# Fourier layer: the feature transform folded a second time, its tables unpacked on ScalarE, and a finer split of the weights

## The chip, the cores and the metric

The kernel runs on one core of a Trainium2 chip. The metric is device time in microseconds (us) of one launch, the median of several runs. Engines are named as in the profile: PE is TensorE (PEld its weight loads), DVE is VectorE, ACT is ScalarE, POOL is GpSimd, SP issues most of the transfers.

## What is computed

Local-global attention on 2 x 8 heads of 768 tokens, then two feed-forward layers. The second one has a two-dimensional Fourier transform ahead of it, of which only the real part is kept; that part is what the change touches.

```python
def _moe2_ref(x, w_ch1, w_ch2):
    X = np.fft.fft(x, axis=1)          # over 768 tokens
    X = np.fft.fft(X, axis=2)          # over 512 features
    u = x + np.real(X).astype(np.float32)
    mu = np.mean(u, axis=-1, keepdims=True)
    var = np.mean((u - mu) ** 2, axis=-1, keepdims=True)
    un = (u - mu) / np.sqrt(var + 1e-06)
    ch = np.maximum(un @ w_ch1, 0.0) @ w_ch2
    return u + ch
```

## The kernel before

**Number format.** Most products run on pairs of fp32r tiles: an operand is split into a rounded part (`h`, `hi`) and a rest (`l`, `lo`), and a product of two operands takes three matmuls: high x high, high x low, low x high. Weights are split in `w_split`: ACT casts 128x1024 values to `wh` (L196), POOL subtracts to get `wo` (L200). For the first 16 chunks POOL does it in four pieces of 256 columns, later in two of 512.

**The main stream.** `ffn` runs over chunks c of 128 hidden units; a block of tokens takes 16 chunks. Chunk c needs 12 products of 512 columns into `ps_h` (L225, "the h pass of c"), then ACT makes `gh` (L232) and DVE makes `gl` (L233), and one chunk later 12 products into four `ps_acc` (L248, "the acc pass of c", which takes `gh`, `gl`, `wh`, `wo` of c). The h pass of c+1 stands ahead of the acc pass of c. At the end of a block DVE adds the accumulators to x (L268).

**Side work.** `drive` advances the main stream step by step (four steps a chunk) and, at a rate given as a number, a chain of side generators; a `yield` is one piece of it. Chunks 16 to 31 carry four transposes and `fft_tables`, chunks 32 to 47 `fft(0)` and the norms, chunks 48 to 63 `fft(1)` and `unit_tokens`. The code's order is not the engines' order: a scheduler places each instruction on its engine, and an instruction that it believes ready may stand ahead of others that were written earlier. On an engine the order is then fixed: an instruction that waits holds all behind it.

**The Fourier part.** `fft(b)` folds the token axis (sums and differences of tokens j and 768-j), and `fold` folds the feature axis once (m and 512-m): 257 cosine terms into `ee`, 256 sine terms into `oo`, split into high and low by ACT (L779) and DVE (L784). Then come products with the token tables `c1` and `s1` (L825 to L849, 386 or 384 columns), split again into `pt` (`fpt`) and `qt` (`fqt`), and products with the feature tables `c2` (258 columns, L862, with one of the sign row `sgn`, L864) and `s2` (256 columns, L875), which sum over two halves `dd` of the features. `pcos` runs four times in an `fft`, the sine products three times. ACT copies the sine result (`qc`, L878); DVE forms `dm` and `sm` (L881, L882) and adds them to x. `c1`, `s1`, `c2`, `s2`, `alt` and `sgn` are loaded by transfers that POOL issues (L739, L742, L751).

Of the kernel before, what the change touches and what calls it, by code (L numbers as in the profile page):

```python
# [39 lines left out]
class Prog:  # L40
# [147 lines left out]
    def w_split(self, c):  # L188
        if c >= PLAIN:
            return  # L190
        nc = self.nc
# [4 lines left out]
        keep(nc.scalar.copy(hi, raw))  # L196

        n = 2 * D // (4 if c < NF else 2)
        for z in range(0, 2 * D, n):
# [553 lines left out]
    def fft(self, b):  # L753
# [11 lines left out]
        oo = fp.tile([P, 2, 3, 256], FR, tag="oo", bufs=1, name=f"oo{b}")  # L765
        ee, oo = [ee[:, z] for z in range(2)], [oo[:, z] for z in range(2)]

        def fold(rows, E, O, h, l, i):
            if O is False:
                f = self.qkb[i % 2][:, 1024:1024 + K1]  # L770
                nc.vector.tensor_tensor(f[0:rows, 1:256], E[:, 1:256], E[:, 511:256:-1], ALU.add)
                nc.vector.tensor_copy(f[0:rows, 0:257:256], E[:, 0:257:256])
                nc.vector.memset(f[0:rows, 257:258], 0.0)
            else:
                f = self.vb[i % 2][:, 1024:1024 + K1]
                nc.vector.tensor_tensor(f[0:rows, 1:256], E[:, 1:256], E[:, 511:256:-1], ALU.subtract)
                nc.vector.memset(f[0:rows, 0:1], 0.0)
            n = K1 if O is False else 256
            nc.scalar.copy(h, f[0:rows, 0:n])  # L779
            if l is None:  # L780
                f, l = f[32:33], h[32:33]
                nc.vector.tensor_tensor(l, f[:, 0:n], l.bitcast(F32), ALU.subtract)
            else:
                nc.vector.tensor_tensor(l, f[0:rows, 0:n], h.bitcast(F32), ALU.subtract)  # L784

        em = fp.tile([P, KP], FR, tag="em", bufs=1, name=f"em{b}")[:, 0:K1]
        for i in range(3):
            E, O = (self.qkb[z][:, (i % 2) * D:(i % 2 + 1) * D] for z in range(2))
            nc.vector.tensor_tensor(E, A[i], Bp[i], ALU.add)
            fold(P, E, False, ee[0][:, i, :], ee[1][:, i, :], i)  # L790
            yield
            nc.vector.tensor_tensor(O, A[i], Bp[i], ALU.subtract)
            fold(P, O, True, oo[0][:, i, :], oo[1][:, i, :], i)
            if i == 1:
                fold(P, xm, False, em, None, 0)
            yield
        if b == 1:
            for _ in range(6):
                yield
        c1, s1, c2, s2 = ([ct[n + "0"], ct[n + "1"]] for n in ("c1", "s1", "c2", "s2"))  # L800
        pt = fp.tile([P, 2, 2, JP], FR, tag="fpt", bufs=1, name=f"fpt{b}")[:, :, :, 0:J1]
# [53 lines left out]
            nc.vector.tensor_tensor(l, pp[:, 0:384], h.bitcast(F32), ALU.subtract)  # L855
            yield

        def pcos(out, at):
            n = 0
            for dd in range(2):  # L860
                for x, y in PS:
                    nc.tensor.matmul(out, lhsT=at(pt[x][:, dd, :]), rhs=c2[y][:, dd, :], start=n == 0, stop=False)  # L862
                    n += 1
            nc.tensor.matmul(out, lhsT=at(pr), rhs=ct["sgn"], start=False, stop=True)  # L864

        for i in range(3):
# [5 lines left out]
            n = 0
            for dd in range(2):
                for x, y in PS:
                    nc.tensor.matmul(qs[:, 0:256], lhsT=qt[x][:, dd, js], rhs=s2[y][:, dd, :], start=n == 0, stop=n == 5)  # L875
                    n += 1
            qc = self.dist[i % 2][:, 2 * K1:3 * K1]
            nc.scalar.copy(qc[:, 0:256], qs[:, 0:256])  # L878
            sm = self.dist[0][:, 0:K1]
            dm = self.dist[0][:, K1:2 * K1]  # L880
            nc.vector.tensor_tensor(dm, pc[:, 0:K1], qc, ALU.subtract)  # L881
            nc.vector.tensor_tensor(sm, pc[:, 0:K1], qc, ALU.add)  # L882
# [417 lines left out]
```

## Time and profile before

| | us |
|---|---|
| median of 3 runs (lowest, highest) | 658.80 (657.76, 659.46) |
| the profiled execution | 660.58 |
| span of the profiled execution | 658.8 |
| PE busy in it | 644.6 |

The profile is of one execution. Its span is from the first to the last instruction; some 1.8 us of the execution lie outside. Busy times of an engine count overlapping instructions once. A matmul's record is longer than the distance to the next one, since matmuls are pipelined: distances between starts are the measure of what one costs.

### The profile page before, as it was taken

The page shows a single profiled execution, that of the slowest core. Times are in us where ns is not written, and L with a number is a line of the kernel's source. Part 1 is how long each engine was busy: PE and PEld are TensorE (multiplying, and loading weights), DVE is VectorE, ACT ScalarE, POOL GpSimd, SP SyncE. Part 2 cuts the span into 40 slices and gives each one's busy share as a digit, 9 for nine tenths or more (in the row PEclk, how much of TensorE's full clock was granted, in tenths as well). Part 3 has the DMA queues.
Part 4 walks back from the last instruction along what each step waited for, and adds up shares of the span by engine and source line. Part 5 has one row for each costly group of instructions (what it writes and reads, how often), then busy time and mean ns, then how long its engine had stood idle before and what let it go on. Part 6 is the DMA issues. An engine that isn't in the chain of part 4 may idle for free.

```text
span 658.8 us, 9571 instructions
## 1 busy us (share of the span) xinstructions
PE 644.6 (98%) x3442; PEld 535.3 (81%) x3442; DVE 425.0 (65%) x784; ACT 298.2 (45%) x584; POOL 345.6 (52%) x360
## 2 busy tenths in 40 slices
PE   6998999999999999999999999999999999999996
PEld 5887777888888888888888888888888888888885
DVE  5799778887839434387467766387556544464544
ACT  5787774554344434335334433235543443233420
POOL 4130235787986554566347665165484664446610
PEclk8999999999999999999999999999999999999999
DMA  7578816788995968666463961112111111011003
GB/s 255 195 302 290 283 44 196 231 262 246 319 352 182 303 221 269 218 198 232 157 202 119 316 223 68 63 65 96 33 64 65 65 64 65 7 58 64 2 2 132
DMA packets 33866, 107.51 MB, mean 163 GB/s; under 512 B 3920, under 2 KB 7952, under 8 KB 30736
## 3 DMA queue, kind: packets, MB, share of 16 engines
q1 hardware_dynamic: 31104, 102.23, 45.7%
q0 software_dynamic: 2416, 3.65, 2.1%
q10 hardware_dynamic: 288, 0.92, 0.4%
q8 instruction: 29, 0.48, 0.3%
q14 instruction: 29, 0.24, 0.1%
HBM read 86.75 MB, written 20.02 MB: 162 GB/s over the span
## 4 chain that ended last, share of the span: by engine, by line
PE 93%; DVE 4%; ACT 1%; issue 0%; DMA 0%; DVEq 0%; POOL 0%; ACTq 0%; POOLq 0%
PE ps_h L225 27%; PE ps_acc L248 27%; PE ps_acc L1060 13%; PE ps_h L1010 10%; PE ps_sd L605 2%; PE ps_acc L537 2%; PE ps_sd L1010 2%; PE ps_sd L580 2%; DVE p L559 2%; PE ps_h L580 1%; PE ps_sd L297 1%; PE ps_sd L825 1%; PE ps_sd L849 1%; PE ps_sd L862 1%; PE ps_sd L875 1%; PE ps_sd L367 1%
## 5 line engine op out<-in xcount | busy, mean ns | idle before, releaser
L200 POOL TENSOR_TENSOR wo<-w,wh 128x512 fp32r<-128x512 f32 (+1 forms) x160 | 207.4, 1321 | 135.7 <-ACT wh L196 122.8
L225 PE MATMUL ps_h<-uT,wh 128*128 128x512 f32 x512 | 131.5, 393 | 0.0
L196 ACT CAST wh<-w 128x1024 fp32r<-128x1024 f32 x64 | 67.3, 1054 | 101.4 <-PE ps_acc L248 55.7
L225 PEld LDWEIGHTS ps_h<-uT,wh 128*128 128x128 f32 x512 | 94.4, 188 | 19.3 <-issue 0.8
L248 PE MATMUL ps_acc<-wh,gh 128*128 128x512 f32 x256 | 101.0, 394 | 0.0
L248 PE MATMUL ps_acc<-wh,gl 128*128 128x512 f32 x256 | 100.0, 391 | 0.0
L248 PE MATMUL ps_acc<-wo,gh 128*128 128x512 f32 x256 | 99.8, 390 | 0.0
L233 DVE SCALAR_TENSOR_TENSOR gl<-ps_h,gh 128x512 fp32r<-128x512 f32 x64 | 43.8, 685 | 74.2 <-ACT gh L232 74.2
L991 POOL TENSOR_TENSOR uo<-ur,uh 128x256 fp32r<-128x256 f32 (+1 forms) x40 | 42.2, 1065 | 59.6 <-ACT uh L988 59.6
L232 ACT ACTIVATE gh<-ps_h 128x512 fp32r<-128x512 f32 x64 | 38.3, 598 | 70.3 <-PE ps_h L225 70.3
L225 PE MATMUL ps_h<-uT,wo 128*128 128x512 f32 x256 | 69.0, 390 | 0.0
L248 PEld LDWEIGHTS ps_acc<-wh,gl 128*128 128x128 f32 x256 | 48.1, 188 | 10.6 <-DVE gl L233 0.3
L1066 DVE TENSOR_TENSOR xall<-ps_acc,xall 128x512 f32<-128x512 f32 x56 | 38.2, 692 | 28.2 <-PE ps_acc L1060 28.2
L225 PEld LDWEIGHTS ps_h<-uT,wo 128*128 128x128 f32 x256 | 48.0, 188 | 10.3
L248 PEld LDWEIGHTS ps_acc<-wo,gh 128*128 128x128 f32 x256 | 48.1, 188 | 9.6 <-issue 0.2
L248 PEld LDWEIGHTS ps_acc<-wh,gh 128*128 128x128 f32 x256 | 48.1, 188 | 9.4 <-issue 0.2
L571 ACT ACTIVATE p<-p,m 128x256 f32<-128x256 f32 (+2 forms) x96 | 47.7, 500 | 9.5 <-DVE m L559 9.5
L169 DVE SCALAR_TENSOR_TENSOR wr<-wr 128x1024 int32<-128x1024 int32 x30 | 44.5, 1483 | 11.1 <-ACT wr L164 10.1
L988 ACT CAST uh<-ur 128x256 fp32r<-128x256 f32 (+1 forms) x40 | 18.8, 488 | 68.7 <-PE ps_acc L1060 62.9
L1010 PE MATMUL ps_h<-op,uh 128*128 128x512 f32 x160 | 49.2, 389 | 0.0
L559 DVE CUSTOM_DVE_ANT_0 p<-ps_acc,dist 128x256 f32<-128x256 f32 (+2 forms) x96 | 35.0, 420 | 7.5 <-PE ps_acc L542 6.8
L1010 PEld LDWEIGHTS ps_h<-op,uh 128*128 128x128 f32 x160 | 30.0, 188 | 6.2
(268 smaller groups left out, 1144.6 us busy)
## 6 DMA issues: line engine op xcount, KB each, us to landing
w<-wscr SPq DMA_DIRECT2D x48, 512.0 KB, 4.0
wr<-wl SPq DMA_DIRECT2D x17, 1024.0 KB, 9.0
wr<-wl SPq DMA_DIRECT2D x60, 256.0 KB, 5.2
wscr<-w SPq DMA_DIRECT2D x16, 512.0 KB, 9.7
wscr<-wd SPq DMA_DIRECT2D x16, 512.0 KB, 2.8
ur<-wscr SPq DMA_DIRECT2D x16, 512.0 KB, 4.4
qk<-qkg SPq DMA_DIRECT2D x7, 1088.0 KB, 7.8
vb<-vw SPq DMA_DIRECT2D x7, 768.0 KB, 4.4
```

Source lines behind the costliest of these rows:

```text
L169: pin(nc.vector.scalar_tensor_tensor(lo, hi, 3, lo, ALU.logical_shift_left, ALU.bitwise_or))
L196: keep(nc.scalar.copy(hi, raw))
L200: keep(nc.gpsimd.tensor_tensor(lo[:, z:z + n], raw[:, z:z + n], hi[:, z:z + n].bitcast(F32), ALU.subtract))
L225: nc.tensor.matmul(hp, lhsT=w[:, dd * P:(dd + 1) * P], rhs=u[:, dd, :], start=n == 0, stop=n == 11)
L232: nc.scalar.activation(gh, hp, AF.Relu)
L233: nc.vector.scalar_tensor_tensor(gl, hp, 0.0, gh.bitcast(F32), ALU.max, ALU.subtract)
L248: nc.tensor.matmul(acc[t], lhsT=g[:, s], rhs=w[:, D:2 * D], start=pf == 0 and m == 0, stop=pf == NF - 1 and m == 2)
L559: keep(nc.vector.tensor_tensor_reduce(out=T[z][:, s], in0=sp[z][:, s], in1=self.dist[z][:, dcol[t]:dcol[t] + width[t]], op0=ALU.add, op1=A ...
L571: keep(nc.scalar.activation(T[z][:, s], T[z][:, s], AF.Exp, bias=m[:, z, y:y + 1], scale=-1.0, accum_out=sm[:, u % 2, y, z:z + 1]))
L991: nc.gpsimd.tensor_tensor(lo[:, s], src, hi[:, s].bitcast(F32), ALU.subtract)
L1010: keep(nc.tensor.matmul(out, lhsT=x[:, s], rhs=y[:, kt, :], start=start and kt + n == 0, stop=kt + n == 3, skip_group_check=not start))
L1060: keep(nc.tensor.matmul(acc[t], lhsT=x[:, s], rhs=y[:, w], start=first and n == 0, stop=not first and n == 2))
```

## The change

`fold` folds the feature axis twice: the even and the odd outputs of the feature transform are sums and differences of m and 256-m. The terms of one half now serve the even outputs and those of the other half the odd ones. So `c2` and `s2` have 130 columns for each half (`KH`) in place of 258 or 256 for both, each product with them has 130 columns, and the number of products stays: 28 with `c2` or `sgn` and 18 with `s2` in an `fft`, 92 in all. The results stand in two halves of a bank, and `dm` and `sm` are written with a stride of two to interleave them. The whole tables are loaded into a raw tile first (`raw2`; for `s2` the first row apart), and ACT copies each second column out, 8 copies of 129 columns, 8 pieces later in the code. The `fold` has more and shorter DVE operations. `w_split` uses four pieces of 256 columns in every chunk. The side rates of the second and the fourth stretch go from 0.30 to 0.38 and from 1.33 to 1.40, and `fft(1)` has 8 empty pieces behind its folds instead of 6. Two small memsets of POOL in each `fft` are gone.

```diff
-        n = 2 * D // (4 if c < NF else 2)
+        n = 2 * D // 4
         for z in range(0, 2 * D, n):
             keep(nc.gpsimd.tensor_tensor(lo[:, z:z + n], raw[:, z:z + n], ...

     def fft_tables(self):
-        for n in ("c1", "s1", "c2", "s2"):
+        for n in ("c1", "s1"):
             for z in range(2):
-                nc.gpsimd.dma_start(ct[f"{n}{z}"], a[f"{n}{z}"][:, :, 0:256] if n == "s2" else a[f"{n}{z}"])
+                nc.gpsimd.dma_start(ct[f"{n}{z}"], a[f"{n}{z}"])
                 yield
+        raw, place = {}, self.fp.tile([P, 2, 2, JP], FR, tag="fpt", bufs=1, name="raw2")
+        for n in ("c2", "s2"):
+            for z in range(2):
+                r, src, row = place[:, z, int(n == "s2"), 0:K1], a[f"{n}{z}"], int(n == "s2")
+                raw[n, z] = r
+                nc.gpsimd.dma_start(r[row:P, :], src[row:P, 0, :])
+                if row:
+                    nc.gpsimd.dma_start(r[0:1, :], src[0:1, 1, :])
+            yield
         nc.gpsimd.memset(ct["alt"][64:128, :].bitcast(F32), 0.0)
         nc.gpsimd.dma_start(ct["alt"][0:64, :], a["alt"])
-        yield
+        for _ in range(8):
+            yield
+        for (n, z), r in raw.items():
+            t = ct[f"{n}{z}"]
+            nc.vector.memset(t[:, :, KH - 1:KH].bitcast(F32), 0.0)
+            for y in range(2):
+                nc.scalar.copy(t[:, y, 0:KH - 1], r[:, y:K1:2])
+            yield

         def fold(rows, E, O, h, l, i):
             if O is False:
...
+                nc.vector.tensor_tensor(f[:, 1:256], E[0:rows, 1:256], E[0:rows, 511:256:-1], ALU.add)
+                nc.vector.tensor_copy(f[:, 0:257:256], E[0:rows, 0:257:256])
+                nc.vector.tensor_tensor(g[:, 0:128], f[:, 0:128], f[:, 256:128:-1], ALU.add)
+                nc.vector.tensor_tensor(f[:, 0:128], f[:, 0:128], f[:, 256:128:-1], ALU.subtract)
             else:
...
+                nc.vector.tensor_tensor(g[:, 0:128], f[:, 0:128], f[:, 256:128:-1], ALU.subtract)
+                nc.vector.tensor_tensor(g[:, 128:256], f[:, 0:128], f[:, 256:128:-1], ALU.add)
+                nc.vector.tensor_copy(g[:, 128:129], f[:, 128:129])
+            nc.scalar.copy(h, g)
...
         if b == 1:
-            for _ in range(6):
+            for _ in range(8):
                 yield
...
-        def pcos(out, at):
-            n = 0
-            for dd in range(2):
-                for x, y in PS:
-                    nc.tensor.matmul(out, lhsT=at(pt[x][:, dd, :]), rhs=c2[y][:, dd, :], ...)
-            nc.tensor.matmul(out, lhsT=at(pr), rhs=ct["sgn"], start=False, stop=True)
+        def pcos(pc, at):
+            for t, out in enumerate(halves(pc)):
+                for n, (x, y) in enumerate(PS):
+                    nc.tensor.matmul(out, lhsT=at(pt[x][:, t, :]), rhs=c2[y][:, t, :], ...)
+                if t == 0:
+                    nc.tensor.matmul(out, lhsT=at(pr), rhs=ct["sgn"][:, 0:KH], start=False, stop=True)
...
-        drive(main, 64, chain(pg.tr_gen(0, range(8, 12), pg.x), pg.fft_tables()), 0.3)
+        drive(main, 64, chain(pg.tr_gen(0, range(8, 12), pg.x), pg.fft_tables()), 0.38)
...
-                              pg.unit_tokens()), 1.33)
+                              pg.unit_tokens()), 1.40)
```

ACT around chunks 15 to 17, before (`wh16` is the high part of the weights of chunk 16, `gh15` the activations of chunk 15):

```order
L196 CAST wh15_2115<-w15_2080 128x1024
L232 ACTIVATE gh14_2137<-ps_h_2124 128x512
L196 CAST wh16_2153<-w16_2122 128x1024
L232 ACTIVATE gh15_2173<-ps_h_2160 128x512
L196 CAST wh17_2203<-w17_2158 128x1024
```

and of the changed kernel:

```order
L196 CAST wh15_2115<-w15_2080 128x1024
L232 ACTIVATE gh14_2137<-ps_h_2124 128x512
L759 COPY c20_2200<-raw2_2508 128x129 x2
L759 COPY c21_2201<-raw2_2508 128x129
L196 CAST wh16_2153<-w16_2122 128x1024
L759 COPY c21_2201<-raw2_2508 128x129
L759 COPY s20_2202<-raw2_2508 128x129 x2
L759 COPY s21_2203<-raw2_2508 128x129 x2
L232 ACTIVATE gh15_2175<-ps_h_2162 128x512
L196 CAST wh17_2205<-w17_2160 128x1024
```

The eight copies of the tables, written 8 pieces behind the transfers, stand right behind `gh14`: three of them ahead of `wh16`, all ahead of `gh15`. The first copy of each table waits for that table's transfers.

DVE in the folds of `fft(1)`, the last rows up to `gl50`, before (`qk0`, `qk1`, `vb0`, `vb1` hold the folded values; `gl50` is 26 rows behind the adds to x of the block's end):

```order
L789 TENSOR_TENSOR qk0_67<-xall1_186 128x512
L784 TENSOR_TENSOR ee1_3883<-qk1_68,ee1_3883 128x258
L784 TENSOR_TENSOR oo1_3884<-vb1_72,oo1_3884 128x256
L782 TENSOR_TENSOR em1_3885<-qk0_67,em1_3885 1x258
L792 TENSOR_TENSOR qk1_68<-xall1_186 128x512
L771 TENSOR_TENSOR qk0_67<-qk0_67 128x255
L772 COPY qk0_67<-qk0_67 128x2
L773 MEMSET qk0_67 128x1
L776 TENSOR_TENSOR vb0_71<-qk1_68 128x255
L777 MEMSET vb0_71 128x1
L233 SCALAR_TENSOR_TENSOR gl50_3985<-ps_h_3971,gh50_3984 128x512
```

and of the changed kernel, where `gl50` is 33 rows behind those adds:

```order
L804 TENSOR_TENSOR ee1_3993<-qk1_68,ee1_3993 128x257
L799 COPY vb1_72<-qk1_68 128x1
L789 COPY qk0_67<-dist1_70 128x2
L809 TENSOR_TENSOR qk0_67<-xall1_186 128x512
L804 TENSOR_TENSOR oo1_3994<-vb1_72,oo1_3994 128x256
L790 TENSOR_TENSOR qk0_67<-qk0_67 128x128
L812 TENSOR_TENSOR qk1_68<-xall1_186 128x512
L792 TENSOR_TENSOR qk0_67<-qk0_67 128x128
L795 TENSOR_TENSOR qk0_67<-qk1_68 128x255
L796 MEMSET qk0_67 128x2
L233 SCALAR_TENSOR_TENSOR gl50_4097<-ps_h_4083,gh50_4096 128x512
```

Between the adds to x and `gl50` there stand 6 operations of 512 columns in both, 12 of 255 to 258 columns before and 10 now, none of 128 columns before and 10 now.

PE at the end of the h pass of chunk 51 (its last products take `wo51`), before:

```order
L225 MATMUL ps_h_4007<-uT100_3601,wo51_3965 128x512 x4
L825 MATMUL ps_sd_4025<-c10_2194,ee1_3883 128x386 x2
L825 MATMUL ps_sd_4025<-c11_2195,ee1_3883 128x386
L825 MATMUL ps_sd_4025<-c10_2194,ee1_3883 128x386
L829 MATMUL ps_sd_4025<-alt_2202,em1_3885 128x386
L248 MATMUL ps_acc_3927<-wh50_3892,gh50_3984 128x512
L248 MATMUL ps_acc_3927<-wo50_3893,gh50_3984 128x512
L248 MATMUL ps_acc_3927<-wh50_3892,gl50_3985 128x512
```

and of the changed kernel:

```order
L225 MATMUL ps_h_4121<-uT100_3687,wo51_4075 128x512 x4
L248 MATMUL ps_acc_4028<-wh50_3977,gh50_4096 128x512
L248 MATMUL ps_acc_4028<-wo50_3978,gh50_4096 128x512
L248 MATMUL ps_acc_4028<-wh50_3977,gl50_4097 128x512
L248 MATMUL ps_acc_4029<-wh50_3977,gh50_4096 128x512
L248 MATMUL ps_acc_4029<-wo50_3978,gh50_4096 128x512
L248 MATMUL ps_acc_4029<-wh50_3977,gl50_4097 128x512
L846 MATMUL ps_sd_4155<-c10_2196,ee1_3993 128x386
```

The ten products with `c1` and `alt` that stood in and behind the h pass of chunk 51 (five in its middle, five at its end) now begin only inside the acc pass of chunk 50, so `gl50` is used directly behind the twelve products of that h pass.

## Rows read from the trace of the kernel before

**Rows 1.** The page: busy time of the engines, and the chain that ended last.

```profile
PE 644.6 (98%) x3442; PEld 535.3 (81%) x3442; DVE 425.0 (65%) x784; ACT 298.2 (45%) x584; POOL 345.6 (52%) x360
...
PE 93%; DVE 4%; ACT 1%; issue 0%; DMA 0%; DVEq 0%; POOL 0%; ACTq 0%; POOLq 0%
```

**Rows 2.** Windows: us, busy us (instructions) by engine, PEclk, DMA share, GB/s.

```profile
11.50:18.30 6.80, 5.16 (x27) 4.77 (x28) 3.35 (x18) 4.54 (x18) 2.09 (x7) 0.50 0.99 384
95.00:490.00 395.00, 394.99 (x1868) 328.36 (x1867) 263.69 (x373) 166.61 (x229) 240.37 (x217) 1.00 0.58 191
```

**Rows 3.** Timeline of PE in fft(0): start, length, line, form, count.

```profile
330.82 0.87 PE L862 MATMUL ps_sd<-c,fpt 128*128 128x258 f32 x6
...
331.65 1.54 PE L225 MATMUL ps_h<-uT,wh 128*128 128x512 f32 x6
333.03 0.89 PE L875 MATMUL ps_sd<-s,fqt 128*128 128x256 f32 x6
333.76 0.63 PE L225 MATMUL ps_h<-uT,wh 128*128 128x512 f32 x2
```

**Rows 4.** Timeline of PE (products of 128 columns) and PEld, fft(1).

```profile
438.73 0.60 PE L942 MATMUL ps_sd<-ident,vb 128*128 128x128 f32 x4
...
439.39 0.40 PE L248 MATMUL ps_acc<-wo,gh 128*128 128x512 f32 x1
...
402.64 0.19 PEld L825 LDWEIGHTS ps_sd<-c,ee 128*128 128x128 f32 x1 [0.33 <-DVE ee L784]
```

**Rows 5.** Groups by line, forms apart: one plain float32 product, in two records.

```profile
L373 PE MATMUL ps_sd<-part,band 128*128 128x512 f32 x2 | 1.0, 590 | 0.0
```

**Rows 6.** Timeline of ACT: gh of chunk 14, wh of chunk 16.

```profile
182.13 0.59 ACT L232 ACTIVATE gh<-ps_h 128x512 fp32r<-128x512 f32 x1
185.95 1.05 ACT L196 CAST wh<-w 128x1024 fp32r<-128x1024 f32 x1 [3.23 <-DMA w<-wscr]
```

**Rows 7.** Timeline of POOL: issues of the tables' transfers, and splits of weights.

```profile
179.96 1.12 POOL L739 DMA_DIRECT2D s<-s  x2
182.32 2.82 POOL L200 TENSOR_TENSOR wo<-w,wh 128x256 fp32r<-128x256 f32 x4 [1.25 <-ACT wh L196]
185.09 1.46 POOL L739 DMA_DIRECT2D c<-c  x2
186.55 1.43 POOL L739 DMA_DIRECT2D s<-s  x2
```

**Rows 8.** Transfers issued from 176 to 200 us: KB each, us to landing.

```profile
s<-s POOLq DMA_DIRECT2D x2, 576.0 KB, 8.9
...
c<-c POOLq DMA_DIRECT2D x2, 258.0 KB, 7.1
...
s<-s POOLq DMA_DIRECT2D x2, 256.0 KB, 10.0
```

**Rows 9.** Timeline of PE at four places.

```profile
13.14 1.66 PE L537 MATMUL ps_acc<-qk 64*128 64x128 f32 x8 [3.18 <-POOL qk L493]
...
189.85 1.98 PE L225 MATMUL ps_h<-uT,wh 128*128 128x512 f32 x8
...
305.78 0.39 PE L248 MATMUL ps_acc<-wh,gl 128*128 128x512 f32 x1
...
398.31 1.53 PE L225 MATMUL ps_h<-uT,wh 128*128 128x512 f32 x6
```

**Rows 10.** Timeline of DVE in the folds of fft(0) and fft(1).

```profile
304.10 0.69 DVE L233 SCALAR_TENSOR_TENSOR gl<-ps_h,gh 128x512 fp32r<-128x512 f32 x1
...
389.14 1.78 DVE L792 TENSOR_TENSOR qk<-xall 128x512 f32<-128x512 f32 x1
...
392.35 0.41 DVE L776 TENSOR_TENSOR vb<-qk 128x255 f32<-128x255 f32 x1
...
401.58 0.68 DVE L233 SCALAR_TENSOR_TENSOR gl<-ps_h,gh 128x512 fp32r<-128x512 f32 x1
```

**Rows 11.** Timeline of POOL beside the second row of Rows 10.

```profile
388.81 3.27 POOL L200 TENSOR_TENSOR wo<-w,wh 128x512 fp32r<-128x512 f32 x2 [2.91 <-ACT wh L196]
```

More of the change, by code (lines that the diff above doesn't have):

```diff
@@ L27 @@
 K1 = 258
-JP, KP = 416, 288
+JP, KP, KH = 416, 288, 130
 KW = S + (NT - 1) * P
@@ L726, in fft_open @@
         self.ct = {}
-        shapes = [(f"{n}{z}", shape, w) for n, shape, w in (("c1", [3, JP], J1), ("s1", [3, 384], 384), ("c2", [2, KP], K1),
-                                                            ("s2", [2, 256], 256)) for z in range(2)]
+        shapes = [(f"{n}{z}", shape, w) for n, shape, w in (("c1", [3, JP], J1), ("s1", [3, 384], 384)) for z in range(2)]
+        shapes += [(f"{n}{z}", [2, KH], KH) for n in ("c2", "s2") for z in range(2)]
         shapes += [("alt", [JP], J1)]
@@ L758, in fft @@
         nc.gpsimd.memset(xm, 0.0)
-        for z in range(2):
-            nc.gpsimd.memset(self.dist[z][:, 3 * K1 - 2:3 * K1], 0.0)
         for r in (0, 32):
@@ L769, in fold @@
             if O is False:
[L770 to L773, printed above, removed]
-            else:
[L775 to L779, printed above, removed]
+                g, f = (self.qkb[i % 2][0:rows, o:o + 257] for o in (1024, 1152))
+                nc.vector.tensor_tensor(f[:, 1:256], E[0:rows, 1:256], E[0:rows, 511:256:-1], ALU.add)
+                nc.vector.tensor_copy(f[:, 0:257:256], E[0:rows, 0:257:256])
+                nc.vector.tensor_tensor(g[:, 0:128], f[:, 0:128], f[:, 256:128:-1], ALU.add)
+                nc.vector.tensor_tensor(f[:, 0:128], f[:, 0:128], f[:, 256:128:-1], ALU.subtract)
+            else:
+                f, g = self.qkb[i % 2][0:rows, 1600:1857], self.vb[i % 2][0:rows, 1024:1280]
+                nc.vector.tensor_tensor(f[:, 1:256], E[0:rows, 1:256], E[0:rows, 511:256:-1], ALU.subtract)
+                nc.vector.memset(f[:, 0:257:256], 0.0)
+                nc.vector.tensor_tensor(g[:, 0:128], f[:, 0:128], f[:, 256:128:-1], ALU.subtract)
+                nc.vector.tensor_tensor(g[:, 128:256], f[:, 0:128], f[:, 256:128:-1], ALU.add)
+                nc.vector.tensor_copy(g[:, 128:129], f[:, 128:129])
+            nc.scalar.copy(h, g)
             if l is None:
[L781 to L784, printed above, removed]
+                g, h = g[32:33], h[32:33]
+                l = h
+            nc.vector.tensor_tensor(l, g, h.bitcast(F32), ALU.subtract)
         em = fp.tile([P, KP], FR, tag="em", bufs=1, name=f"em{b}")[:, 0:K1]
@@ L789, in fft @@
             nc.vector.tensor_tensor(E, A[i], Bp[i], ALU.add)
[L790 removed]
+            fold(P, E, False, ee[0][:, i, 0:257], ee[1][:, i, 0:257], i)
             yield
@@ L856, in fft, with halves, both, inter @@
             yield
-        def pcos(out, at):
-            n = 0
-            for dd in range(2):
-                for x, y in PS:
-                    nc.tensor.matmul(out, lhsT=at(pt[x][:, dd, :]), rhs=c2[y][:, dd, :], start=n == 0, stop=False)
-                    n += 1
-            nc.tensor.matmul(out, lhsT=at(pr), rhs=ct["sgn"], start=False, stop=True)
+        def halves(pc):
+            return [pc[:, y * 256:y * 256 + KH] for y in range(2)]
+        def pcos(pc, at):
+            for t, out in enumerate(halves(pc)):
+                for n, (x, y) in enumerate(PS):
+                    nc.tensor.matmul(out, lhsT=at(pt[x][:, t, :]), rhs=c2[y][:, t, :], start=n == 0, stop=t == 1 and n == 2)
+                if t == 0:
+                    nc.tensor.matmul(out, lhsT=at(pr), rhs=ct["sgn"][:, 0:KH], start=False, stop=True)
+        def both(pc):
+            return pc.rearrange("p (t k) -> p t k", t=2)[:, :, 0:KH]
+        def inter(v):
+            return v.rearrange("p (k t) -> p t k", t=2)
+        sm, dm = (self.dist[0][:, z * 2 * KH:(z + 1) * 2 * KH] for z in range(2))
         for i in range(3):
@@ L868, in fft @@
             pc = self.psum("m")
-            pcos(pc[:, 0:K1], lambda m: m[:, js])
+            pcos(pc, lambda m: m[:, js])
             yield
             qs = self.psum("m2")
[L872 to L882, printed above, removed]
+            for t, out in enumerate(halves(qs)):
+                for n, (x, y) in enumerate(PS):
+                    nc.tensor.matmul(out, lhsT=qt[x][:, t, js], rhs=s2[y][:, t, :], start=n == 0, stop=n == 2)
+            qc = self.dist[i % 2][:, 4 * KH:6 * KH].rearrange("p (t k) -> p t k", t=2)
+            nc.scalar.copy(qc, both(qs))
+            nc.vector.tensor_tensor(inter(dm), both(pc), qc, ALU.subtract)
+            nc.vector.tensor_tensor(inter(sm), both(pc), qc, ALU.add)
             for X, lo_, hi_ in ((A[i], dm, sm), (Bp[i], sm, dm)):
@@ L887, in fft @@
         pc = self.psum("m")
-        pcos(pc[:, 0:K1], lambda m: same(m[:, 384:385]))
+        pcos(pc, lambda m: same(m[:, 384:385]))
+        nc.scalar.copy(inter(sm[0:1]), both(pc[0:1]))
         X = Bp[0]
-        nc.vector.tensor_tensor(X[0:1, 0:257], pc[0:1, 0:257], xm[0:1, 0:257], ALU.add)
-        nc.vector.tensor_tensor(X[0:1, 511:256:-1], pc[0:1, 1:256], xm[0:1, 511:256:-1], ALU.add)
+        nc.vector.tensor_tensor(X[0:1, 0:257], sm[0:1, 0:257], xm[0:1, 0:257], ALU.add)
+        nc.vector.tensor_tensor(X[0:1, 511:256:-1], sm[0:1, 1:256], xm[0:1, 511:256:-1], ALU.add)
         yield
```

3 lines of the change are left out of this document (2 added, 1 removed).

## Prediction

> **What bounds the kernel now.** I read the chain of waits first, because it says which engine's time is the kernel's time: PE holds 93% of it, and DVE, ACT and POOL are busy for 65, 45 and 52% [rows 1]. Then the windows, since a mean over the span hides stages: from 95 to 490 us, where everything that the change touches lies, PE is busy for 394.99 of 395 us at a granted clock of 1.00 [rows 2]. So a microsecond less of matmuls there is a microsecond less of time, a microsecond in which PE stands is one more, and what happens on another engine counts only if PE comes to wait for it. Three questions follow: what the narrow products cost PE, which operands of PE come later than now, and by how much they were early.
>
> **A. The narrow products (all on the path).** 92 products go from 258 or 256 columns to 130. A record is longer than its share, so I take distances between starts. In fft(0), six products with c2 and one with sgn go from 330.82 to 331.65, 0.83 / 7 = 0.119 each; six with s2 from 333.03 to 333.76, 0.122 each [rows 3]. With 56 of the first kind and 36 of the second the mean is 0.1196. A product of 512 columns takes (1.98 - 0.39) / 7 = 0.227 [rows 9], so a column costs (0.227 - 0.119) / 254 = 0.00043, and 130 columns alone would cost 0.065: 92 x 0.055 = 5.1 us less. But each product needs its own 128-column weight load. Four products of 128 columns and one of 512 take 439.39 - 438.73 = 0.66 [rows 4]; less 0.227 that is 0.108 each, nearly twice what their columns explain. These are transposes, not fp32r products, but load and columns are as many. I take 0.108: 92 x (0.1196 - 0.108) = **-1.1 us**. The lower end is -5.1. The upper end: no row shows an fp32r product under 256 columns. The nearest that is slower is a plain float32 product, whose two records of 512 columns take 1.0 us [rows 5], so 130 columns take 0.25 and the sum is 92 x 0.13 = +12.0.
>
> The Trainium skill (TensorE: Matmul & The Clock Gate, Back-to-back issue gap) gives 81 ns per product for a stream of loads and matmuls of 128 columns; the 0.108 of rows 4 speaks against it. By the page the term would be 92 x (0.1196 - 0.081) = -3.6 and the sum below 659.8, inside the range.
>
> **B. The copies of the tables on ACT.** Before, ACT does gh14 at 182.13 to 182.72, then waits for the weights of chunk 16 and casts wh16 from 185.95 to 187.00 [rows 6]; PE starts h(16), which reads it, at 189.85 [rows 9]. So wh16 is 2.85 early. Now three copies stand ahead of wh16 and all eight ahead of gh15, and the first waits for c20's transfer. POOL still issues these transfers behind the split that ends at 185.1: c2 from 185.09, s2 from 186.55 [rows 7]. Their queue still carries the second s1 transfer, issued about 180.5 (the second of two from 179.96) [rows 7], which lands 8.9 us later, at 189.4 [rows 8]. Before, the c2 transfers landed at 185.09 + 7.1 = 192.2 and 0.7 later, 2.8 and 3.5 behind s1's, and the s2 ones at 196.6 and 197.3 [rows 7, 8]. With half the bytes I halve these distances: c20 at 190.8, c21 at 191.15, s2 at 193.0 to 193.35. A copy of 129 columns is about 0.25 (0.59 for 512 columns and 1.05 for 1024 [rows 6], so 0.46 for 512 more, 0.34 less for 383 fewer than 512). Then c20's two copies and one of c21 end at 191.55, wh16 at 192.6, and h(16) starts 2.8 late: **+2.8 us**. gh15 follows the s2 copies at 194.0 to 194.6; PE needs it behind the twelve products of h(16), at 192.6 + 2.7 = 195.3, so it adds nothing. POOL has wh16 at 192.6 and splits the half that h(16) wants in 1.4 (half of 2.82 [rows 7]), at 194.0; PE wants it behind eight products, at 194.4: nothing either. Low end: c2 lands together with s1, at 189.4, then 1.4. High end: transfers land as before, at 192.2 and 196.6: h(16) 4.3 late and gh15 1.6 more, 5.9.
>
> **C. The folds of fft(1) on DVE.** Ahead of gl50 stand ten operations of 128 columns more and two of some 256 fewer. From 0.69 (512 columns) and 0.41 (255) [rows 10] a 128-column one has a record of about 0.27, and some 0.07 of a record overlaps the next, so 10 x 0.2 - 2 x 0.33 = +1.4. gl50 ended at 401.58 + 0.68 = 402.26 [rows 10] and now ends at about 403.7. What needs it comes earlier: the ten products with c1 and alt stood in and behind h(51) and now follow. h(51) starts at 398.31 [rows 9]; the third product of acc(50) stands 14 products behind that start, at 398.31 + 14 x 0.227 = 401.5. PE waits 403.7 - 401.5 = **+2.2 us**. The wait of 0.33 that the first of those ten products has for `ee` now [rows 4] is gone, since they stand behind the wait for gl50: **-0.3**. Low end 0: in these folds an operation of 512 columns takes 1.78 instead of 0.69 [rows 10] beside POOL's split of 3.27 [rows 11], 1.1 lost; two such losses may fall elsewhere now. High end 3.3: one more of them falls into the folds, as POOL's four pieces make more starts.
>
> **D. The folds of fft(0).** gl35 ends at 304.79 [rows 10], and PE wants it at 305.78 [rows 9]: 0.99 to spare. The DVE order puts part of the new operations ahead of it, about +0.9: nothing, with 0 to 1.8 as bounds (C's loss of 1.1 more).
>
> **E. Costed at nothing.** Splits in four pieces: 2.82 for four [rows 7] against 3.27 for two in a bad place [rows 11]; POOL is idle for half the span and its weights are early, while without that cover 48 splits at some 0.3 would be 14 us. The transfers that POOL issues more often (two, 0.7 each by rows 7) stand ahead of a split that ACT's wh16 holds anyway. The rates, the empty pieces, the strided dm and sm, the longer turn of a psum buffer and the removed memsets move work beside a PE that has other products to do: 0, at most 0.6.
>
> **Sum.** -1.1 + 2.8 + 2.2 - 0.3 = +3.6 us. The profiled execution (span 658.8, 660.58 in all) lies 1.8 above the median of 658.8; it would become 664.2. The difference goes onto the median: **662.4 us**.
>
> **The rivals.** 1) *The load hides behind the product that runs* (not slower). If in a row of fp32r products the load of the next goes on while the columns of this one stream, A is up to -5.1 and not -1.1: 658.4. For it: the products before take no more than their columns plus 0.01. Against: rows 4. It decides from a period under 0.085, where A reaches -3.2 and the sum falls to +1.5, inside 0.3%.
> 2) *The transfers are early enough, or ACT isn't held.* Without B the sum is +0.8: 659.6. For it: half the bytes, and 185.1 to 189.85 is 4.7 us. Against: transfers of this queue take 7.1 to 10.0 us [rows 8], and s1 lands at 189.4.
> 3) *PE's clock falls in the new wait.* At 13.14 PE had stood for 3.18 us [rows 9], and in the stretch round it, 11.5 to 18.3, the granted clock is 0.50 [rows 2], the 1.2 GHz level. A wait of 2.8 at h(16) is nearly as long; 6.8 us at half clock cost 3.4: 665.8. Against: PE was fully busy for 95 us before it.
> 4) *Products under 256 columns run at the plain float32 rate.* +12.0 for -1.1: 675.5. No row speaks for it but the absence of any narrower fp32r product.
>
> **How the numbers follow.** A difference under 0.3% (2.0 us) can't be told from none: faster is below 656.8, slower above 660.8. Forecast 0.50, spread over 659.5 to 665 by the ends of B and C, with 0.07 of it below 660.8; rival 1 0.13, of which 0.05 with small B or C ends faster; rival 2 0.12, within 0.3% but for 0.01 faster and 0.02 slower; rival 3 0.12, slower; rival 4 0.13, slower. Faster 0.05 + 0.01 = 0.06; same 0.07 + 0.08 + 0.09 = 0.24; slower 0.70. The range takes in the forecast and rivals 1 to 3, from 657.5 to 667.0, and leaves out rival 4 (0.13) and the far ends of B, C and rival 1 (0.06).
>
> **What would show it.** A: distances between starts of the products with c2 and s2, 0.108 (rival 1: near 0.07; rival 4: 0.2 and more). B: ACT idle from gh14 to about 190.8 with the raw transfers as releaser, and PE standing for 2.8 before h(16); without such a wait B falls. C: PE standing near 401 for gl50, 2 us; if gl50 ends by 401.5, C falls. Rival 3: a granted clock under 1.00 between 190 and 205. D and E: no other wait of PE over 0.6 from 95 to 490. I am wrong if PE's busy time in the products changes by more than 2 us, or if a wait stands at a place that isn't named here.

## The result: 1.4% slower, by a wait on ACT and the clock behind it

| | before | changed |
|---|---|---|
| median, us (runs) | 659.13 (4) | 669.28 (4) |
| ratio to before, 95% interval | | 1.0141 (1.0123 to 1.0159) |
| profiled execution's span | 658.8 | 668.5 |
| PE busy in it | 644.6 | 647.5 |

The forecast was 662.4, with 667.0 as the upper end of its range: the sign was right, the size was not. (The ratio is estimated from all runs; the two medians alone give 1.0154.) PE is still what the time follows, but its share of the chain of waits fell from 93% [rows 1] to 67%. The page of the changed kernel:

```profile
PE 647.5 (97%) x3442; PEld 535.8 (80%) x3442; DVE 435.2 (65%) x816; ACT 300.8 (45%) x594; POOL 371.3 (56%) x454
...
PE 67%; DVE 7%; ACT 2%; DMA 1%; POOL 0%; issue 0%; DVEq 0%; ACTq 0%
```

Starts of the h passes, which both traces have at the same places of the program, tell where the difference arose. The stretch ahead of h(15) varies from run to run (h(15) started between 1.9 us earlier and 0.2 later than in the profile before, in all the traces below), so I count from there:

| stretch | changed less before, us |
|---|---|
| ahead of h(15) (not touched by the change) | -0.35 |
| h(15) to h(16): the wait on ACT | +4.86 |
| h(16) to h(20): PE at half clock | +2.98 |
| h(20) to h(48), with fft(0) | -0.63 |
| h(48) to h(63), with fft(1) | +2.67 |
| behind h(63) | +0.17 |
| sum (668.5 - 658.8) | +9.7 |

**The wait and the clock.** The timeline of ACT round chunk 16, to be held against [rows 6] (a copy is shown as a CAST):

```profile
181.79 0.59 ACT L232 ACTIVATE gh<-ps_h 128x512 fp32r<-128x512 f32 x1
192.28 0.51 ACT L759 CAST c<-raw 128x129 fp32r<-128x129 f32 x2 [9.90 <-DMA raw<-c]
193.06 0.31 ACT L759 CAST c<-raw 128x129 fp32r<-128x129 f32 x1 [0.27 <-DMA raw<-c]
193.27 1.04 ACT L196 CAST wh<-w 128x1024 fp32r<-128x1024 f32 x1
194.22 0.30 ACT L759 CAST c<-raw 128x129 fp32r<-128x129 f32 x1
194.42 0.93 ACT L759 CAST s<-raw 128x129 fp32r<-128x129 f32 x4
195.26 0.58 ACT L232 ACTIVATE gh<-ps_h 128x512 fp32r<-128x512 f32 x1
```

ACT stands for 9.90 us with the raw table's transfer as releaser, and wh16 ends at 194.31 where it ended at 187.00 [rows 6]. POOL issues the transfers when it did before [rows 7]; what they took is in the list of transfers issued from 176 to 200 us (KB each, us to landing):

```profile
raw<-c POOLq DMA_DIRECT2D x2, 129.0 KB, 7.6
raw<-s POOLq DMA_DIRECT2D x2, 128.0 KB, 7.4
```

For c2 half the bytes did not land earlier: 7.6 us against the 7.1 of 258 KB. s2, which lands behind it, did: 7.4 against 10.0 [rows 8]. Ahead of both the same queue carries s1; its second transfer by itself, before and then changed:

```profile
s<-s POOLq DMA_DIRECT2D x1, 576.0 KB, 9.9
```

```profile
s<-s POOLq DMA_DIRECT2D x1, 576.0 KB, 10.4
```

It landed at 190.5 before (issued at 180.5) and at 190.6 now (issued at 180.2), so c20 landed 1.7 us behind it in both. PE, which needs wh16, in its timeline, and then the windows of that stretch (us, busy by engine, granted clock as the third number from the end):

```profile
189.27 0.39 PE L248 MATMUL ps_acc<-wh,gl 128*128 128x512 f32 x1
194.36 3.78 PE L225 MATMUL ps_h<-uT,wh 128*128 128x512 f32 x8 [4.70 <-ACT wh L196]
```

```profile
194.36:200.30 5.94, 5.94 (x14) 4.68 (x15) 0.69 (x1) 2.83 (x8) 5.85 (x10) 0.50 0.61 210
200.30:205.00 4.70, 4.70 (x23) 3.83 (x23) 4.48 (x8) 2.87 (x4) 0.85 (x2) 0.98 0.02 3
```

From start to start 5.09 us, 4.86 more than one product. Behind it the clock is granted at 0.50, the 1.2 GHz level, for 5.94 us. That costs half of them, 2.97, and the table has 2.98 there.

**The folds of fft(1).** The timelines of PE (four rows), DVE and ACT near gl50 and ee, to be held against [rows 4] and [rows 10]:

```profile
408.11 0.39 PE L248 MATMUL ps_acc<-wo,gh 128*128 128x512 f32 x1
410.48 0.50 PE L248 MATMUL ps_acc<-wh,gl 128*128 128x512 f32 x1 [1.98 <-DVE gl L233]
...
413.78 0.34 PE L846 MATMUL ps_sd<-c,ee 128*128 128x386 f32 x1
414.88 0.91 PE L846 MATMUL ps_sd<-c,ee 128*128 128x386 f32 x3 [0.76 <-ACT ee L800]
```

```profile
409.75 0.68 DVE L233 SCALAR_TENSOR_TENSOR gl<-ps_h,gh 128x512 fp32r<-128x512 f32 x1
...
414.86 0.43 DVE L804 TENSOR_TENSOR ee<-qk,ee 128x257 fp32r<-128x257 f32 x1
```

```profile
414.42 0.41 ACT L800 CAST ee<-qk 128x257 fp32r<-128x257 f32 x1 [0.28 <-DVE qk L792]
```

The wait for gl50 costs 410.48 - 408.11 - 0.23 = 2.14; the next one, which no step of the prediction had, 414.88 - 413.78 - 0.18 = 0.92. Behind neither does the clock fall in this trace.

**The narrow products.** The first group of them in fft(0), to be held against [rows 3]:

```profile
338.08 0.45 PE L886 MATMUL ps_sd<-c,fpt 128*128 128x130 f32 x3
338.36 0.28 PE L888 MATMUL ps_sd<-sgn,fpr 128*128 128x130 f32 x1
338.47 0.50 PE L886 MATMUL ps_sd<-c,fpt 128*128 128x130 f32 x3
338.81 1.59 PE L225 MATMUL ps_h<-uT,wh 128*128 128x512 f32 x6
340.24 0.78 PE L905 MATMUL ps_sd<-s,fqt 128*128 128x130 f32 x6
```

Seven products take 338.81 - 338.08 = 0.73 instead of 0.83 [rows 3]. But the first of them takes only 0.06, and the second wide product behind the group starts 0.28 after the first and not 0.23: what the first narrow one seems to gain, the wide one gives back. With that added, the 92 products take 10.31 us, before 11.14: 0.112 each instead of 0.121. The weight loads of the same group tell why:

```profile
338.30 0.19 PEld L888 LDWEIGHTS ps_sd<-sgn,fpr 128*128 128x128 f32 x1
338.41 0.42 PEld L886 LDWEIGHTS ps_sd<-c,fpt 128*128 128x128 f32 x3
338.75 1.22 PEld L225 LDWEIGHTS ps_h<-uT,wh 128*128 128x128 f32 x6
```

They start 0.11 us apart, and the first load of the wide products behind them keeps that distance.

### The profile page after: what moved, and what is told of

Same layout as the page of the kernel before. It is cut to its first block, busy times and chain, and to the rows that moved or that the text cites. A ratio compares the mean times of both kernels' runs of the same rounds, so it can differ in the third digit from the quotient of the medians.

```text
span 668.5 us, 9705 instructions
## 1 busy us (share of the span) xinstructions
PE 647.5 (97%) x3442; PEld 535.8 (80%) x3442; DVE 435.2 (65%) x816; ACT 300.8 (45%) x594; POOL 371.3 (56%) x454
## 3 DMA queue, kind: packets, MB, share of 16 engines
q0 software_dynamic: 1968, 3.13, 1.9%
## 4 chain that ended last, share of the span: by engine, by line
PE 67%; DVE 7%; ACT 2%; DMA 1%; POOL 0%; issue 0%; DVEq 0%; ACTq 0%
PE ps_h L225 19%; PE ps_acc L248 19%; PE ps_acc L1088 13%; PE ps_h L1038 10%; DVE wr L169 2%; PE ps_sd L1038 2%; DVE w L171 2%; ACT wh L196 1%; DMA raw<-c 1%; PE ps_sd L870 1%; ACT wr L164 1%; PE ps_sd L846 1%; PE ps_sd L297 1%; PE ps_sd L886 1%; PE ps_sd L905 1%; DVE qk L788 0%
## 5 line engine op out<-in xcount | busy, mean ns | idle before, releaser
L200 POOL TENSOR_TENSOR wo<-w,wh 128x256 fp32r<-128x256 f32 x256 | 232.8, 940 | 124.1 <-ACT wh L196 101.1
L225 PE MATMUL ps_h<-uT,wh 128*128 128x512 f32 x512 | 134.0, 398 | 4.7 <-ACT wh L196 4.7
```

Source lines behind the costliest of these rows:

```text
L225: nc.tensor.matmul(hp, lhsT=w[:, dd * P:(dd + 1) * P], rhs=u[:, dd, :], start=n == 0, stop=n == 11)
```

## The experiments

Theory: ACT's copies hold wh16 until the raw tables land, PE waits for it, and its clock falls behind the wait; the folds, longer on DVE, give the rest. Rivals: the transfers collide with the weights' whatever ACT does; the clock falls for another reason; the narrow products cost what they seemed to gain. Comparisons by median are with runs of the kernel before on the same chip.

### Without the copies

The tables are stored packed, as the products read them; nothing else differs from the changed kernel.

```diff
-        raw, place = {}, self.fp.tile([P, 2, 2, JP], FR, tag="fpt", bufs=1, name="raw2")
         for n in ("c2", "s2"):
             for z in range(2):
-                r, src, row = ...
+                nc.gpsimd.dma_start(ct[f"{n}{z}"], a[f"{n}{z}"])
...
-            for y in range(2):
-                nc.scalar.copy(t[:, y, 0:KH - 1], r[:, y:K1:2])
```

> The changed kernel, with the tables c2 and s2 stored packed in memory (two halves of 130 columns each), so that the transfers land in the tables and ACT's eight copies and the raw tile are gone; all else, the folds, the narrow products, the splits and the rates, as changed. Theory (the wait for the copies on ACT holds wh16, and PE's clock falls behind it): PE's wait of 4.9 us ahead of h(16) and the 3.0 us that the products behind it lost at half clock both go, about 7.8 us less than the changed kernel, 661.5 us, and the granted clock is 1.00 from 180 to 205 us. Left over the kernel before: about +2.3, from the waits of 2.2 for gl50 and 0.9 for ee near 410 us, less 0.8 from the narrow products. Rival (the transfers collide with the weights' and the copies only show it): wh16 or its weights stay late, and 3 us or more of the wait stay, 664 us or more.

Measured: 661.78 us, ratio 1.0041 (1.0025 to 1.0058). Its PE timeline has h(16) directly behind its forerunner, and the two waits of fft(1) as in the changed kernel:

```profile
189.33 1.98 PE L225 MATMUL ps_h<-uT,wh 128*128 128x512 f32 x8
...
402.52 0.50 PE L248 MATMUL ps_acc<-wh,gl 128*128 128x512 f32 x1 [1.99 <-DVE gl L233]
...
406.92 0.91 PE L837 MATMUL ps_sd<-c,ee 128*128 128x386 f32 x3 [0.77 <-ACT ee L791]
```

The granted clock is 1.00 throughout from 189 to 206 us. So the copies' wait, with the clock behind it, is 7.5 us by the medians (7.7 with each kernel against its own runs of the kernel before), 7.8 by the h starts (h(15) to h(20)): three quarters of the loss. The collision of transfers falls as a rival, since these transfers are issued at the same place.

### The wait alone, in the kernel before

```diff
         nc.gpsimd.dma_start(ct["alt"][0:64, :], a["alt"])
+        hold = self.cp.tile([P, 2], F32, name="hold")
+        for _ in range(8):
+            yield
+        nc.scalar.copy(hold, ct["c20"][:, 0, 0:2].bitcast(F32))
```

The copy stands between gh14 and wh16 on ACT, as the table copies do. e4 reads s11, which lands earlier.

> The kernel before, with one copy of two columns of the table c20 on ACT between gh14 and wh16, so that wh16 waits for c20's transfer; nothing else is changed. Theory (ACT's wait for a table alone gives the loss, without any fold): c20 lands at about 192.2, wh16 ends at about 193.4, h(16) starts 3.6 us late; PE's clock falls behind this wait and costs some 3 us more: +6.5 us over the kernel before, 665.5. Rival (the clock keeps its level behind a wait of this length): +3.6, 662.7. Second rival (other work covers the hold): within 0.5 us of the kernel before.

> The kernel before, with the same copy on ACT between gh14 and wh16, but of two columns of the table s11, whose transfer lands earlier. Theory: s11 lands between 189.4 (by the median time to landing) and 190.9 (where the changed kernel's queue stood), wh16 ends at 190.6 to 192.1, PE waits 0.7 to 2.2 us and keeps its clock, as it did behind the 2.0 us wait near 410 us of the changed kernel: +0.7 to +2.2 us. Rival (the clock falls behind any wait of PE at this place): +3.5 us or more.

Measured: e3 668.45 us, ratio 1.0139 (1.0099 to 1.0179); e4 664.87, ratio 1.0083 (1.0064 to 1.0102). Both are more than expected, but not at this place. By the h starts e3 loses 3.18 us in the wait and 1.73 behind it, e4 1.32 and 0.14. That is in kind what the theories said, though e3's clock cost 1.7 and not some 3; another 3.5 us (3.3 in e4) come in the last stage, 300 us behind the copy. There PE does fewer products in the same time, first the kernel before, then e3 (the windows; the instructions of PE in brackets):

```profile
520.00:640.00 120.00, 120.00 (x532) 99.38 (x531) 62.14 (x88) 41.99 (x86) 59.16 (x65) 1.00 0.10 36
```

```profile
520.00:640.00 120.00, 120.00 (x520) 97.32 (x519) 63.36 (x89) 41.24 (x86) 60.29 (x67) 1.00 0.12 39
```

It stands nowhere in either; each product takes 0.231 and not 0.227. Two more kernels looked for the cause: e8 makes the added tile 64 bytes wide, e11 adds no tile and lets the copy write into columns of the tile of `alt` that nothing reads.

> e3_hold_c2 again, with the tile that takes ACT's copy 64 bytes wide and not 8 (two of its 16 columns are written). In e3 and e4 the 704 products of the last stage (its L1014 and L1064) took 0.231 and not 0.227 each, 3.5 us in sum, though the copy is 300 us earlier; the 8 bytes move all tiles allocated behind. Theory (the place of the operands in memory makes these products slower): they take 0.227 again, and the time is the kernel before plus the wait and the clock of the trace of e3 alone, 3.2 + 1.7 = 4.9 us, 664.2. Rival (the hold itself slows the last stage): 667 us and 0.231 again.

> e3_hold_c2 again, with ACT's copy written into columns of the table alt's tile that nothing reads, so that no tile is added and none moves. If the place of the tiles makes the last stage's 704 products slower (0.231 in e3 and e8), they take 0.227 here, and the time is the kernel before plus 4.9 to 5.3 us, about 664.4. If the hold itself does, they take 0.231 and the time is 668 again.

Measured: e8 668.55 us, ratio 1.0142 (1.0114 to 1.017), and 521 products in these 120 us; e11 664.8, ratio 1.0082 (1.0063 to 1.0102), and 531. So the added tile made the last stage slow, and my guess in e8, that 64 bytes leave the others where they do no harm, was wrong. e11 is the clean measure of the hold: ACT, PE and the window behind:

```profile
190.50 0.19 ACT L746 CAST alt<-c 128x2 fp32r<-128x2 f32 x1 [9.21 <-DMA c<-c]
190.60 1.04 ACT L196 CAST wh<-w 128x1024 fp32r<-128x1024 f32 x1
```

```profile
191.69 3.52 PE L225 MATMUL ps_h<-uT,wh 128*128 128x512 f32 x8 [3.13 <-ACT wh L196]
```

```profile
191.70:195.50 3.80, 3.80 (x10) 3.01 (x11) 0.69 (x1) 1.36 (x2) 3.72 (x5) 0.55 0.95 307
```

3.29 us in the wait and 1.75 behind it by the h starts, 5.0 in sum; the median says 5.2. No fold, no narrow product and no raw tile is in this kernel: a hold on ACT alone gives the wait and the fall of the clock. In e4 PE's wait is 1.16 and the clock stays at 1.00.

### The price of the narrow products

The products of e1 are made 256 columns wide.

```diff
-            return [pc[:, y * 256:y * 256 + KH] for y in range(2)]
+            return [pc[:, y * 256:y * 256 + 256] for y in range(2)]
```

> As e1_direct, but each product with c2, s2 and sgn has 256 columns and not 130: the tables are padded with columns of zeros, and the results in the further columns are not used. Theory (a product costs the larger of its weight load, 0.112, and its columns): 92 products from 0.112 to 0.121, 0.8 us more than e1_direct. Rival (columns alone, 0.00043 us each): 92 x 126 x 0.00043 = 5.0 us more than e1_direct.

Measured: 662.62 us, ratio 1.0042 (1.0026 to 1.0057), 0.84 above e1's median. The same group as above (its first product and the wide one behind it):

```profile
329.83 0.52 PE L877 MATMUL ps_sd<-c,fpt 128*128 128x256 f32 x3
...
330.65 1.55 PE L225 MATMUL ps_h<-uT,wh 128*128 128x512 f32 x6
```

0.82 for seven, near the 0.83 of [rows 3]; all 92 take 11.00 us, 0.69 more than the narrow ones. The columns alone would have made it 5.0 more; that rival falls. The 0.84 between the medians is not a clean price: it compares two chips (0.76 with each kernel against its own runs of the kernel before), and in e7's profiled execution something else differs too. Its wait for gl50 is as long as the changed kernel's, but here the clock falls behind it (the wait, then a window):

```profile
402.63 0.50 PE L248 MATMUL ps_acc<-wh,gl 128*128 128x512 f32 x1 [1.98 <-DVE gl L233]
```

```profile
403.40:407.00 3.60, 3.60 (x11) 3.15 (x10) 3.50 (x8) 0.86 (x3) 3.20 (x5) 0.53 0.00 0
```

That costs about 1.5 us, and the wait for `ee` behind it, which PE now reaches later, is gone. So a wait of 2 us has been seen with either clock.

### The folds

e2 puts the ten products with c1 and alt back to where the kernel before had them.

```diff
-        drive(main, 64, chain(pg.tr_gen(0, range(8, 12), pg.x), pg.fft_tables()), 0.38)
+        drive(main, 64, chain(pg.tr_gen(0, range(8, 12), pg.x), pg.fft_tables()), 0.3)
...
-            for _ in range(8):
+            for _ in range(6):
...
-                              pg.unit_tokens()), 1.40)
+                              pg.unit_tokens()), 1.33)
```

> As e1_direct (tables stored packed), and with the side rates 0.30 and 1.33 and the six empty pieces of the kernel before, so that ten products with c1 and alt stand again in and behind h(51), ahead of the products that need gl50. Theory (gl50 is about 1.4 us later on DVE, and the other part of its wait is that those ten products no longer cover it): the wait for gl50 near 400 us falls from 2.2 to about 0.5, a wait for ee takes up to 1 us, about 1.5 us less than e1_direct, 660 us. Rival (DVE's folds alone set it: the products wait for the folds' own results wherever they stand): no change against e1_direct within 0.5 us.

Measured: 666.09 us, ratio 1.0105 (1.0088 to 1.0122), 4.3 above e1. Both expectations are wrong:

```profile
406.35 1.33 PE L837 MATMUL ps_sd<-c,ee 128*128 128x386 f32 x3 [5.75 <-ACT ee L791]
```

```profile
406.50:412.50 6.00, 6.00 (x19) 5.29 (x20) 1.51 (x3) 0.78 (x2) 0.56 (x2) 0.60 0.26 87
```

Three of the ten read the third block of `ee`, most of whose fold DVE now does behind gl50; ahead of acc(50) they wait for it 5.75 us, and the clock falls again (0.60 in the 6 us behind). The place that the change gives these products is what keeps this from happening. The price of that place is that they no longer cover gl50. This part is worked out and not measured: in e2 gl50 ends at 401.96, and without the wait for `ee` PE would want it at about 401.6 (400.27 + 5 x 0.18 + 2 x 0.23), a wait of 0.3 and not 2.

e5 gives the folds more room: two more empty pieces behind each half, two instead of eight behind them all. e6 also works in place (three small copies fewer on DVE) and folds the odd row last; e12 uses e6's in-place form with three more pieces and the rate 1.55.

> As e1_direct (tables stored packed), with two more empty pieces behind each half of the folds of fft(1) and only two empty pieces behind them all, so that DVE does gl50 behind 27 operations and not 33, and the products with c1 start a chunk later. Theory (gl50 queued behind the folds on DVE, and ee not ready, are what PE waits for near 400 us): gl50 comes about 1.7 us earlier, its wait falls from 2.2 to about 0.5, the wait for ee (0.9) goes: about 2.6 us less than e1_direct, 659.2 us, no more than the kernel before within 0.3%. Rival (the folds' work on DVE sets the end of this stretch, not its place): the wait moves to the next products and e1_direct's time stays within 0.8 us.

> As e5_spread, with the first fold of the sums done in place (three copies of two columns on DVE gone) and the fold of the odd row behind the last block and not the second, so that gl50 stands behind 22 operations. Theory: no wait of PE over 0.3 us is left near 400 us; 0.5 us less than e5_spread, 658.7 us, which is the kernel before less the narrow products' 0.8, 0.1% faster. Rival (small operations on DVE are free): the same as e5_spread within 0.3 us.

> e1_direct with the first fold of the sums in place, three more empty pieces behind each half of the folds of fft(1), none behind them all, and the rate 1.55 in place of 1.40. gl50 stands behind 25 operations and gl51 behind 40 (e5: 27 and 43), and the products with c1 begin half a chunk later. Theory (the folds' queue on DVE and ACT is what PE waits for; e5 and e6 left 1.3 and 1.6 us of waits near 406 us and 0.6 at 489): the waits near 400 us fall to 0.8, that at 489 goes, 660.3 us. Rival (the folds' work finds no free place on DVE): the waits move again and 662 us or more remain.

Measured: e5 662.25, ratio 1.004 (1.0023 to 1.0056); e6 662.78, ratio 1.0049 (1.0032 to 1.0065); e12 660.93, ratio 1.0023 (1.0012 to 1.0034). The waits of PE that are left in e5, then in e6, then in e12:

```profile
400.94 0.50 PE L248 MATMUL ps_acc<-wh,gl 128*128 128x512 f32 x1 [0.27 <-DVE gl L233]
...
406.91 0.50 PE L248 MATMUL ps_acc<-wh,gh 128*128 128x512 f32 x1 [0.67 <-ACT gh L232]
...
408.00 0.50 PE L248 MATMUL ps_acc<-wh,gl 128*128 128x512 f32 x1 [0.36 <-DVE gl L233]
...
488.82 0.50 PE L248 MATMUL ps_acc<-wh,gl 128*128 128x512 f32 x1 [0.36 <-DVE gl L233]
```

```profile
407.64 0.50 PE L248 MATMUL ps_acc<-wh,gh 128*128 128x512 f32 x1 [1.58 <-ACT gh L232]
```

```profile
304.31 0.44 PE L841 MATMUL ps_sd<-c,ee 128*128 128x386 f32 x1 [0.56 <-DVE qk L788]
...
407.64 0.50 PE L248 MATMUL ps_acc<-wh,gl 128*128 128x512 f32 x1 [0.85 <-DVE gl L233]
```

gl50 is cured (0.27 instead of 1.99), and the wait comes back one chunk later: gh51 stands on ACT behind the high parts of folds, which wait for DVE. In e5 the rival was right, the time is e1's. e6's in-place form gains nothing (658.7 was expected), keeps a wait of 0.36 for `gl` at 489 us, and brings a wait of 0.56 into fft(0) (e12's first row; e6 has the same). e12 comes out near its theory (660.3; 0.85 is left near 400 us, none at 489). It is the best of the folded-twice kernels, still 0.23% behind the kernel before; none of them beats it.

### POOL's pieces

e9 is the kernel before with four pieces everywhere, e10 is e1 with two behind chunk 16.

```diff
-        n = 2 * D // (4 if c < NF else 2)
+        n = 2 * D // 4
```

> The kernel before with one edit of the change alone: POOL's split of the weights in four pieces of 256 columns in every chunk and not only in the first 16. Theory (POOL is idle for half the span): no wait of PE, within 0.3% of the kernel before. Rival (more pieces mean more turns in which DVE's folds wait): gl50 and ee come later and PE waits up to 1 us near 400 us.

> e1_direct with the split of the weights in two pieces of 512 columns behind the first 16 chunks, as in the kernel before. Theory (DVE and POOL take turns, and a split costs the folds on DVE about its own length however it is cut): the waits near 400 us stay at 3 us in sum, e1_direct's time within 0.8 us. Rival (the four pieces make the folds late): the waits fall by 1 us or more.

Measured: e9 659.34, ratio 0.9994 (0.9982 to 1.0005), no wait of PE from 95 to 490 us; e10 663.43, ratio 1.0056 (1.0039 to 1.0073). In e10 the waits near 400 us are as long as in e1:

```profile
403.46 0.50 PE L248 MATMUL ps_acc<-wh,gl 128*128 128x512 f32 x1 [2.04 <-DVE gl L233]
408.09 0.94 PE L837 MATMUL ps_sd<-c,ee 128*128 128x386 f32 x3 [0.99 <-ACT ee L791]
```

The four pieces cost nothing and do not make the folds late. The 1.6 us between e10's and e1's medians (1.4 with each kernel against its own runs of the kernel before) are above the 0.8 that the theory allowed; 1.2 of it shows in the traces: 0.3 near 400 us, 0.2 in fft(0), 0.7 behind h(63), more than half of it a wait for `gl` at 488 us. The intervals overlap, and I do not settle it.

## Why the prediction was wrong, point by point

- **A, narrow products, -1.1: right.** -0.83 by the distances; e7, 256 columns wide, gives 0.69 of it back. The period is 0.112, the load's, and not 0.108. The rivals 1 (-5.1) and 4 (+12.0) fall. Two slips carry no weight: the mean before is 0.1198 by the rows, and with a term of -3.6 the sum is 659.9.
- **B, the copies, +2.8: the place and the chain were right, the size failed, at c2's landing.** ACT's first copy began at 192.28 and not 190.8, wh16 ended at 194.31 and not 192.6, and h(16) was 4.86 late. Two steps of the prediction made the 1.5. "With half the bytes I halve these distances": c20 landed 1.7 behind s1 before and now, which is about 1.0 of it. And "lands 8.9 us later, at 189.4" took the middle of two transfers (7.8 and 9.9) for the second: s1 landed at 190.5, so the distance that was halved was 1.7 and not 2.8, which is the other 0.5. The prediction's own high end, "transfers land as before", had 192.2 and 4.3: it was the better row to take, since it was measured and the halving was not. It is not that bytes never count on this queue: s2, with half of them, landed in 7.4 instead of 10.0, and e1 (130 KB) against e7 (256 KB) shows the same, 7.1 and 7.0 for c2, 7.2 and 8.8 for s2. What sets c2's landing, no run here shows. Of the 0.5 between 4.3 and 4.86, 0.35 is that all of this execution ran that much earlier up to the tables' issue, while c2 landed when it had before; the rest is in c21's landing and ACT's copies.
- **Rival 3, the clock, +3.4: happened, +2.98, the largest term that the sum lacked.** It stood as a case beside the forecast, with a chance of 0.12. The argument against it, "PE was fully busy for 95 us before it", did not hold: PE has no wait between 95 us and h(16) in the changed kernel either, and the clock fell. In these traces it fell with each wait of 3 us and more: 3.02 (e3), 3.13 (e11, 1.75 us lost), 3.40 (e8), 4.70 (the changed kernel, 2.98) and 5.75 (e2). It stayed behind 1.16 (e4). Near 2 us it did both: it stayed in the changed kernel, e1 and e10 (1.98 to 2.04) and fell in e7 (1.98). So the length of a wait alone does not settle it, and whether the forecast's 2.8 would have been paid twice stays open. The high end of B should have carried the clock with it, 5.9 + 3.4, which would have put the range's end at 668.9 (-1.1 + 5.9 + 3.4 + 2.2 - 0.3 = +10.1) and not at 667.0; the measured 669.28 lies 0.4 above even that.
- **C, gl50, +2.2: right,** 2.14, and in both parts: h(48) starts 6.86 later than before by the table, so gl50 ended 1.3 later (410.43 - 6.86 = 403.57 for 402.26; 1.4 was forecast), and its product was due at 401.5 (408.11 + 0.23 - 6.86). **The -0.3 beside it was wrong:** the old wait for `ee` went, as said, but a new one of 0.92 came, for the third block's `ee`. The step "they stand behind the wait for gl50" looked only at the products' own place; most of the third block's fold on DVE had gone from ahead of gl50 to behind it (in the changed kernel its last row ends 4.9 us behind gl50, before 0.3 us), so it was the later of the two.
- **D and E, 0: right** for the folds of fft(0), where PE has no wait, and for the pieces (e9). The rates and empty pieces, also in E, are not nothing on this path: e2, which takes them back, costs 4.3.
- **Sum by measured terms:** -0.83 + 4.86 + 2.98 + 2.14 + 0.92 - 0.33 = +9.7, where the spans differ by 9.7 and the h starts from h(15) on by 10.05; 0.3 are in places too small to name. Of the 6.1 that the forecast lacked, 2.98 are the clock, 2.06 B's size, 0.92 the new wait for `ee` and 0.27 A. Both of its own signs of being wrong came: PE's busy time rose by 2.9 us, and the wait for `ee` stands where none was named.

## What to carry to other kernels

An engine that is half idle still holds what is queued behind one waiting instruction: ask of each added copy where a scheduler will put it, what its operand's transfer last took to land (from the row of that transfer alone, not the middle of several, and not scaled by bytes), and who needs the instruction behind it. Price a wait of the bounding engine together with the clock behind it, since a wait may be paid twice: here all five of 3 us and more were, and one of four near 2 us. And narrowing a product below the time of its weight load gives nothing: look at the distance between loads before folding further.

## What the runs showed that was not expected

- For c2, half the bytes and the same landing: 129 KB in 7.6 us, 258 KB in 7.1, on the same queue at the same place. For s2 behind it, 128 KB in 7.4 and 256 KB in 10.0.
- The clock behind a wait of 2 us: 1.00 in three kernels, 0.53 over 3.6 us in e7. What decides it stays open.
- A tile of 8 or 64 bytes added to a pool that outlives the stage made products 300 us later slower, 0.231 for 0.227 us each (520 and 521 instead of 532 in 120 us, 3.5 us over the stage), with no wait and the clock at 1.00. Without the tile it was gone (e11). Which operand's place does it stays open.
- A narrow product at a group's head takes 0.06 us, and the wide product behind the group pays 0.05 more.
